# Attention feeding a SwiGLU block: the combined tile half a group later, q and k by DMA from tile 9, a new pace for attention

## The chip, the cores and the metric

The kernel runs on one core of a Trainium2 chip. The metric is device time in microseconds (us) of one execution, lower is better. Where a few tenths matter I also quote the mean granted TensorE clock of a run: a run at a mean clock of 0.99 is not the same run as one at 1.00.

## The reference, cut to what matters

Eight batches of eight heads, 576 positions, head size 64. Attention looks back over a window of 128 positions with a linear bias; its output, 4608 tokens of 512 values, goes through a gated feed-forward block.

```python
def _attn_ref(q, k, v):                       # (8, 8, 576, 64) each
    scores = scale * np.matmul(q, k.transpose(0, 1, 3, 2))
    bias = slopes[:, None, None] * (-np.abs(rel))[None, :, :]
    mask = (rel >= 0) & (rel < 128)
    scores = np.where(mask, scores + bias[None], -1e9)
    ...                                       # softmax over the keys
    return np.matmul(attn, v)

def _moe_ref(x, w_gate, w_val, w_out):        # x (4608, 512), 512 -> 1536 -> 512
    g = x @ w_gate
    silu = g * (1.0 / (1.0 + np.exp(-g)))
    return silu * (x @ w_val) @ w_out
```

## The kernel before: the parts concerned

The work is one stream of TensorE (PE) instructions in which attention and feed-forward are interleaved. Two batches form a group `s`. A group has eight whole tiles of 128 rows (p = 0 to 7) and one *combined* tile (p = 8) that holds the last 64 rows of both batches. Attention makes the tiles in the order of `units`; the feed-forward block takes them 512 rows at a time (blocks 0 to 7, and block 8 of the four combined tiles).

```python
QK_DMA_FROM = 14                 # q and k of tiles from here on are transposed by DMA
...
units = [(s, p) for s in range(NSUP) for p in range(9)]
...
def transpose(n):
    name, rank = order[n]
    if rank < QK_DMA_FROM:
        transposed(name, rank)   # 4 PE transposes and a copy by VectorE or ScalarE
        return
    t_ = (natk if name == "k" else natq).pop(rank)
    nc.sync.dma_start_transpose(transposed_home(name, rank), t_.rearrange("p h d -> p (h d)"))
```

The scores of tile p take its own keys against its own queries and those of the next tile, so scores of (1,0) need q of two tiles:

```python
nc.tensor.matmul(two[par][:, j, :], kT[rows, ks, pair, :],
                 qT[rows, p:p + 2, pair, :], start=(j == 0), stop=(j == 1))
```

Loads of q, k and v are issued by GpSimd into one queue, through a ring of four buffers each for q and k (`nat`, `bufs=4`). A load waits for the transpose that reads its buffer. The two halves of the output weight (768 KB each) stand in the same queue, behind tile 8.

How far attention runs is set by the step of the feed-forward block:

```python
for step in steps:
    if step < 24:
        blk, target = 0, base + max(0, step - ALONE) + 2 * max(0, step - 16)
    else:
        blk = min(NBLK - 1, 1 + int((step + LEAD - 24) // 34.5))
        target = base + 32 + (step - 24) * RATE * 8 / 34.5
    while (n_att < target or done < ready[blk]) and att_step():
        pass
```

The softmax here doesn't subtract the row's maximum and nothing guards it: scores larger than these inputs give would overflow.

## Time and profile before

| what | before |
|---|---|
| time, median of 3 runs | 361.49 us |
| span of the profiled run | 359.7 us, mean clock 0.997 |
| PE busy | 343.1 us (95%) |
| idle PE between 27 and 351 us | 6.6 us |
| longest PE wait after the start | 1.49 us, at 54.43 us, just before block 1 |

The lines behind this table stand in the prediction. The row of slices for the granted clock (40 slices of 9.0 us, a 9 is 90% or more): full until the drain. PE's timeline: start, duration, engine, line, operation, and in brackets the idle time before it with what ended it.

```profile
PEclk9999999999999999999999999999999999999998
```

### The profile page before, as it was taken

How to read it: one execution, taken by the hardware profiler on the slowest of the kernel's cores; microseconds unless marked ns; L12 is line 12 of the kernel's file. 1: busy time of each engine (PE TensorE's matmuls, PEld its weight loads, DVE VectorE, ACT ScalarE, POOL GpSimd, SP SyncE). 2: the span in 40 equal slices, each digit the busy share in tenths (PEclk: the TensorE clock that was granted, in tenths of full speed). 3: DMA queues.
4: the chain of work that ended last, by engine and by line, in shares of the span. 5: the costliest groups of instructions: out<-in, count | busy, mean ns of one | idle time of the engine just before them, and what ended most of it. 6: DMA issues, size and time to landing. Idle time of an engine off the chain costs nothing.

```text
span 359.7 us, 7185 instructions
## 1 busy us (share of the span) xinstructions
PE 343.1 (95%) x2741; PEld 196.1 (55%) x2741; DVE 273.9 (76%) x599; ACT 180.3 (50%) x356; POOL 106.8 (30%) x132
## 2 busy tenths in 40 slices
PE   7888989999999999999999999999999999999995
PEld 3654445444556655565566655564565566456543
DVE  4748975987987799768977998789877955975540
ACT  4837675456755555456565454555454333333321
POOL 8954778325153165463560001000000000000000
PEclk9999999999999999999999999999999999999998
DMA  9999999969999999999999303220031101101113
GB/s 149 171 187 186 172 178 149 134 46 112 107 119 98 110 117 136 185 170 142 175 179 175 89 18 29 84 78 16 15 76 55 49 10 51 58 2 59 60 25 93
DMA packets 154499, 36.55 MB, mean 102 GB/s; under 512 B 144992, under 2 KB 149984, under 8 KB 154464
## 3 DMA queue, kind: packets, MB, share of 16 engines
q0 software_dynamic: 116224, 18.62, 79.6%
q1 hardware_dynamic: 37792, 17.18, 24.6%
q8 instruction: 21, 0.34, 0.4%
q10 hardware_dynamic: 448, 0.30, 0.3%
q14 instruction: 14, 0.11, 0.1%
HBM read 37.91 MB, written 9.44 MB: 132 GB/s over the span
## 4 chain that ended last, share of the span: by engine, by line
PE 72%; DVE 8%; DMA 7%; ACT 5%; POOL 4%; issue 3%; ACTq 0%; DVEq 0%; POOLq 0%
PE pg L361 21%; PE pv L361 21%; PE po L470 14%; PE av L312 4%; DMA qn<-in_q_dram 4%; PE po L391 3%; PE ps L252 3%; PE p L470 2%; DMA wv_sb<-in_moe_w_val_dram 2%; PE px L338 2%; DVE uu L374 2%; ACT ex L257 1%; DVE hT L378 1%; ACT tt L372 1%; PE psc L280 1%
## 5 line engine op out<-in xcount | busy, mean ns | idle before, releaser
L372 ACT ACTIVATE tt<-pg 128x512 f16<-128x512 f32 x108 | 64.8, 602 | 112.8 <-PE pg L361 104.9
L361 PE MATMUL pg<-xT,wg_sb 128*128 128x512 f16 (+2 forms) x444 | 114.9, 373 | 1.0 <-ACT xT L339 0.7
L361 PE MATMUL pv<-xT,wv_sb 128*128 128x512 f16 (+2 forms) x444 | 113.6, 373 | 0.5 <-DVE uu L374 0.5
L374 DVE SCALAR_TENSOR_TENSOR uu<-tt,pg 128x512 f16<-128x512 f16 x107 | 73.0, 683 | 34.8 <-ACT tt L372 34.6
L378 DVE TENSOR_TENSOR hT<-uu,pv 128x512 f16<-128x512 f16 x108 | 73.7, 683 | 6.9 <-PE pv L361 3.9
L361 PEld LDWEIGHTS <-wg_sb 128*128 128x128 f16 x444 | 41.7, 98 | 40.2 <-issue 3.8
L361 PEld LDWEIGHTS <-wv_sb 128*128 128x128 f16 x444 | 41.0, 98 | 35.4 <-issue 3.1
L257 ACT ACTIVATE ex<-ps 128x512 f16<-128x512 f32 x96 | 50.4, 608 | 10.9 <-PE ps L252 10.8
L172 POOL DMA_DIRECT2D qn<-in_q_dram x39 | 33.3, 858 | 40.9 <-DMA qT<-qn 34.3
L166 POOL DMA_DIRECT2D va<-in_v_dram x40 | 34.0, 857 | 35.5 <-PE av L312 27.4
L172 POOL DMA_DIRECT2D kn<-in_k_dram x39 | 33.2, 854 | 32.6 <-DMA kT<-kn 25.2
L470 PEld LDWEIGHTS <-hT 128*128 128x128 f16 x336 | 32.0, 98 | 15.5 <-issue 2.3
L261 DVE TENSOR_TENSOR ex<-ex,m_reg 128x1024 f16<-128x1024 f16 x48 | 32.7, 687 | 7.5 <-ACT ex L257 7.2
L470 PEld LDWEIGHTS <-S 128*128 128x128 f16 x252 | 23.9, 98 | 13.4 <-issue 4.9
L315 DVE TENSOR_TENSOR x<-av,rec 128x256 f16<-128x256 f32 x72 | 29.0, 420 | 0.8
L470 PE MATMUL po<-T,S 128*128 128x256 f16 x168 | 23.1, 273 | 0.1
L470 PE MATMUL po<-T,hT 128*128 128x256 f16 x168 | 22.9, 272 | 0.2 <-DVE osb L474 0.2
L284 ACT ACTIVATE exc<-psc 128x512 f16<-128x512 f32 x40 | 21.2, 608 | 3.3 <-PE psc L280 3.3
L312 PE MATMUL av<-va,ex 128*128 128x65 f16 x384 | 20.7, 193 | 1.8 <-DVE x L315 1.3
L312 PEld LDWEIGHTS <-ex 128*128 128x128 f16 x384 | 18.1, 97 | 6.0 <-DVE x L315 2.0
L339 ACT COPY xT<-px 128x512 f16<-128x512 f16 x24 | 14.0, 584 | 13.7 <-PE px L338 13.3
L391 PE MATMUL po<-wo_sb,hT 128*128 128x512 f16 x84 | 20.7, 379 | 0.0
(72 smaller groups left out, 295.6 us busy)
## 6 DMA issues: line engine op xcount, KB each, us to landing
out_dram<-osb SPq DMA_DIRECT2D x32, 256.0 KB, 2.2
va<-in_v_dram POOLq DMA_DIRECT2D x32, 128.0 KB, 7.7
qn<-in_q_dram POOLq DMA_DIRECT2D x31, 128.0 KB, 6.7
kn<-in_k_dram POOLq DMA_DIRECT2D x31, 128.0 KB, 6.3
wo_sb<-in_moe_w_out_dram POOLq DMA_DIRECT2D x2, 768.0 KB, 9.1
wg_sb<-in_moe_w_gate_dram POOLq DMA_DIRECT2D x2, 512.0 KB, 10.6
wv_sb<-in_moe_w_val_dram POOLq DMA_DIRECT2D x2, 512.0 KB, 12.3
out_dram<-osb SPq DMA_DIRECT2D x6, 128.0 KB, 2.3
```

The source lines that it names most:

```text
L166: nc.gpsimd.dma_start(va[rank][p0:p1, :, 0:D], src)
L172: nc.gpsimd.dma_start(t_[p0:p1], src)
L257: nc.scalar.activation(e[:, o:o + 2, :], banks[q4][par], AF.Exp, scale=scale)
L261: nc.vector.tensor_mul(e[:, o, :], e[:, o, :], reg[:, o, :])
L312: nc.tensor.matmul(av[:, j, :], w, val, start=(n == 0), stop=(n == len(todo) - 1))
L315: nc.vector.tensor_mul(x[:, 4 * half:4 * half + 4, :], av[:, :, 0:D], rec.broadcast_to([P, 4, D]))
L361: nc.tensor.matmul(ps[:, c0:c1], w[:, kb, ms], xT[n][:, kb, c0:c1], start=(kb == 0 and c0 == 0), stop=(kb == NKB - 1 and c1 == 512))
L372: nc.scalar.activation(tt, pg, AF.Tanh, scale=0.5)
L374: nc.vector.scalar_tensor_tensor(out=uu, in0=tt, scalar=one if (n, m) == PIN else 1.0, in1=pg, op0=ALU.add, op1=ALU.mult)
L378: nc.vector.tensor_mul(hT[n][:, m, :], uu, pv)
L391: nc.tensor.matmul(po, hT[n][:, m, j * P:(j + 1) * P], wo_sb[:, m, :], start=(i == 0), stop=(i == NMB - 1))
L470: nc.tensor.matmul(dst, a[:, m, cols], b[:, m, :], start=(start and m == 0), stop=(m == HM - 1), skip_group_check=True)
```

## The change

There are four intentions in it. (1) The combined tile of a group moves half a group later, so that block 2 waits for 12 attention tiles instead of 13. (2) q and k of tiles 9 to 13 are transposed by DMA instead of PE, as all later tiles already are. (3) One quarter of block 0's projection (12 matmuls) is put ahead of block 1, as filler, and the rest is spread. (4) Attention gets an even pace in stretches. The rest (homes of the tiles in the rings, shared masks, lists of what is needed when) follows from (1).

```diff
-QK_DMA_FROM = 14
+QK_DMA_FROM = 9
+PRE = 1
+SECOND = 5
...
-    NK, NQ = 12, 9
+    NK, NQ = 14, 10
...
-    opool = ctx.enter_context(tc.tile_pool(name="op", bufs=8))
+    opool = ctx.enter_context(tc.tile_pool(name="op", bufs=7))
...
-    units = [(s, p) for s in range(NSUP) for p in range(9)]
+    units = [(0, p) for p in range(8)]
+    for s in range(1, NSUP):
+        units += [(s, 0), (s, 1), (s, 2), (s, 3), (s - 1, 8), (s, 4), (s, 5), (s, 6), (s, 7)]
+    units += [(NSUP - 1, 8)]
...                                 (homes in the rings, masks, order of the transposes)
+            if n == 1:
+                for j in range(PRE):
+                    for _ in project(0, j, ps_f, "po", 1):
+                        yield 1.0
...
-                    if 1 <= m <= 4:
-                        for _ in project(0, m - 1, ps_f, "po", 1):
+                    if m % 2 and PRE + m // 2 < 4:
+                        for _ in project(0, PRE + m // 2, ps_f, "po", 1):
...
-    ready = [4, 8, 13, 17, 22, 26, 31, 35, 36]
+    ready = [4, 8, 12, 17, 21, 26, 30, 35, 36]
...
-            if step < 24:
-                blk, target = 0, base + max(0, step - ALONE) + 2 * max(0, step - 16)
+            b1 = 24 + 3 * PRE
+            blk = (0 if step + LEAD < b1 else 1 if step + LEAD < 60
+                   else min(NBLK - 1, 2 + int((step + LEAD - 60) // 34.5)))
+            if step < b1:
+                target = base + 32 * max(0, step - ALONE) / (b1 - ALONE)
+            elif step < 60:
+                target = base + 32 + SECOND * 8 * (step - b1) / (60 - b1)
             else:
-                blk = min(NBLK - 1, 1 + int((step + LEAD - 24) // 34.5))
-                target = base + 32 + (step - 24) * RATE * 8 / 34.5
+                target = base + 32 + SECOND * 8 + (step - 60) * RATE * 8 / 34.5
```

Tile numbers count along `units`. In the order of before, tile 8 is the combined tile (0,8) and tile 9 is (1,0). In the new order tile 8 is (1,0), tile 9 is (1,1) and the combined tile (0,8) is tile 12.

More of the change, by code (lines that the diff above doesn't have):

```diff
@@ L97 @@
     nc.vector.memset(idle, 0.0)
-    msk = [consts.tile([P, H, P], FP16, name=f"m_c{n}") for n in range(3)]
-    nc.vector.memset(msk[0][:, :, 64:128], 0.0)
-    nc.vector.memset(msk[1][:, :, 0:64], 0.0)
+    band = consts.tile([P, H, 192], FP16, name="m_band")
+    msk = [band[:, :, 64:192], band[:, :, 0:128], consts.tile([P, H, P], FP16, name="m_own")]
+    nc.vector.memset(band, 0.0)
     nc.vector.memset(msk[2], 0.0)
     def make_masks():
-        nc.scalar.copy(msk[0][:, :, 0:64], reg[:, :, 128:192])
-        nc.scalar.copy(msk[1][:, :, 64:128], reg[:, :, 128:192])
+        nc.scalar.copy(band[:, :, 64:128], reg[:, :, 128:192])
         nc.scalar.copy(msk[2][0:64, :, 0:64], reg[0:64, :, 0:64])
@@ L140 @@
         va_all += [tv[:, 0], tv[:, 1]]
-    units = [(s, p) for s in range(NSUP) for p in range(9)]
+    units = [(0, p) for p in range(8)]
+    for s in range(1, NSUP):
+        units += [(s, 0), (s, 1), (s, 2), (s, 3), (s - 1, 8), (s, 4), (s, 5), (s, 6), (s, 7)]
+    units += [(NSUP - 1, 8)]
+    rank_of = {u: i for i, u in enumerate(units)}
     last = len(units) - 1
@@ L149, with home @@
     natq, natk, va = {}, {}, {}
+    def home(name, s, c):
+        if name == "q":
+            return c if c < 8 else 8 + s % 2
+        if c in (3, 7, 8):
+            return 8 + 3 * (s % 2) + (3, 7, 8).index(c)
+        return (6 * s + (0, 1, 2, 4, 5, 6).index(c)) % 8
     def transposed_home(name, rank):
-        return kT[:, rank % NK] if name == "k" else qT[:, rank % NQ]
+        return (kT if name == "k" else qT)[:, home(name, *units[rank])]
     def source(src, rank):
-        s, c = divmod(rank, 9)
+        s, c = units[rank]
         if c == 8:
@@ L163, in load_v @@
     def load_v(rank):
-        va[rank] = va_all[rank % NV]
+        va[rank] = va_all[home("v", *units[rank])]
         for (p0, p1), src in source(v, rank):
@@ L204, in transposed @@
             nc.vector.tensor_copy(transposed_home(name, rank), pt)
-    order = []
-    for s in range(NSUP):
-        for half in (0, 4):
-            order += [(name, 9 * s + half + r) for name, r in zip("kqqkqkqk", (0, 0, 1, 1, 2, 2, 3, 3))]
-        order += [("k", 9 * s + 8), ("q", 9 * s + 8)]
-    need = [18 * s + n for s in range(NSUP) for n in (3, 5, 7, 8, 11, 13, 15, 18, 18)]
+    order, need = [], []
+    for i, (s, p) in enumerate(units):
+        wanted = [("k", s, p), ("q", s, p)] + ([("q", s, p + 1)] if p not in (3, 7, 8) else [])
+        if i < last and units[i + 1][1] == 8:
+            wanted += [("k", units[i + 1][0], 8), ("q", units[i + 1][0], 8)]
+        order += [w for w in ((n, rank_of[(s_, c)]) for n, s_, c in wanted) if w not in order]
+        need.append(len(order))
     def transpose(n):
@@ L226, in scores, with combined @@
         s, p = units[i]
-        def combined(n):
+        def combined(s, n):
             return scores_128(s, (3, 7, 8)[n], 8, (s, "c", n), msk[n])
@@ L233, in scores @@
         if p == 8:
-            return together(combined(1), combined(2))
-        if p == 7:
-            return together(scores_128(s, p, p, (s, p), reg[:, :, 0:P]), combined(0))
-        if p == 3:
-            return scores_128(s, p, p, (s, p), reg[:, :, 0:P])
-        ks = (9 * s + p) % NK
+            return together(combined(s, 1), combined(s, 2))
+        if p in (3, 7):
+            own = scores_128(s, p, p, (s, p), reg[:, :, 0:P])
+            follows = i < last and units[i + 1][1] == 8
+            return together(own, combined(units[i + 1][0], 0)) if follows else own
+        ks = home("k", s, p)
         banks = []
@@ L266, in scores_128 @@
     def scores_128(s, kt, qt, key, m):
-        ks = (9 * s + kt) % NK
+        ks, qs = home("k", s, kt), home("q", s, qt)
         banks = []
@@ L279, in products @@
                     rows = slice(64 * par, 64 * par + 64)
-                    nc.tensor.matmul(banks[par][:, j, :], kT[rows, ks, j, :], qT[rows, qt, j, :],
+                    nc.tensor.matmul(banks[par][:, j, :], kT[rows, ks, j, :], qT[rows, qs, j, :],
                                      start=(j == 0), stop=(j == 3))
@@ L304, in weighted @@
                     for n, kt in enumerate((3, 7, 8)):
-                        todo.append((j, ex[(s, "c", n)][:, slot(h), :], va[9 * s + kt][:, h, :]))
+                        todo.append((j, ex[(s, "c", n)][:, slot(h), :], va[rank_of[(s, kt)]][:, h, :]))
                 else:
@@ L308, in weighted @@
                         todo.append((j, ex[(s, p - 1)][:, slot(h), 128:256],
-                                     va[9 * s + p - 1][:, h, :]))
-                    todo.append((j, ex[(s, p)][:, slot(h), 0:128], va[9 * s + p][:, h, :]))
+                                     va[rank_of[(s, p - 1)]][:, h, :]))
+                    todo.append((j, ex[(s, p)][:, slot(h), 0:128], va[rank_of[(s, p)]][:, h, :]))
             for n, (j, w, val) in enumerate(todo):
```

## The prediction

> **What bounds the kernel now.** I read the page's first table first, then the slices, then the busy time by stretches, then the waits, and last the timeline of the stretch in which the stretches showed a loss.
>
> ```profile
> PE 343.1 (95%) x2741; PEld 196.1 (55%) x2741; DVE 273.9 (76%) x599; ACT 180.3 (50%) x356; POOL 106.8 (30%) x132
> ...
> DMA  9999999969999999999999303220031101101113
> ```
>
> TensorE is busy 343.1 of 359.7 us, so 16.6 us is all that visible idle time could give. The second line shows where another limit stands: the DMA engines are full for the first half of the run. The stretches say where the 16.6 us lie (columns: stretch, its length, busy PE, PEld, DVE, ACT, POOL, then granted clock, DMA share, GB/s):
>
> ```profile
> 0.00:27.00 27.00, 21.25 (x237) 14.19 (x238) 14.69 (x45) 14.26 (x29) 22.19 (x31) 1.00 1.86 169
> 27.00:54.00 27.00, 24.06 (x204) 12.02 (x201) 23.10 (x47) 19.85 (x39) 17.22 (x22) 1.00 1.86 179
> 54.00:72.00 18.00, 17.36 (x146) 9.03 (x147) 13.89 (x32) 9.06 (x17) 11.19 (x13) 1.00 2.38 141
> 72.00:276.00 204.00, 201.37 (x1668) 115.47 (x1667) 170.89 (x378) 111.80 (x223) 56.17 (x68) 1.00 1.08 101
> 276.00:351.00 75.00, 74.57 (x463) 42.39 (x462) 50.92 (x101) 24.37 (x47) 0.00 (x0) 1.00 0.13 43
> ```
>
> Idle PE: 5.75 us before 27 us (the start, which the change hardly touches), 2.94 from 27 to 54, 0.64 from 54 to 72, 2.63 in the next 204, 0.43 in the next 75, and 4.5 in the drain. So from 27 us on the change can win at most 6.6 us of visible idle time, and none of it for sure. The one large piece is here, at the end of block 0, just before block 1 may begin:
>
> ```profile
> 52.13 0.81 PE L361 MATMUL pv<-xT,wv_sb 128*128 128x512 f16 x3
> 54.43 0.28 PE L338 MATMUL px<-idm,x 128*128 128x128 f16 x2 [1.49 <-DVE x L315]
> ```
>
> PE stands 1.49 us waiting for the attention tile that completes block 1's input. The diff aims at this: it gives attention an even pace and puts 12 projection matmuls of block 0 behind it as filler. In the same stretch the loads are one full queue:
>
> ```profile
> va<-in_v_dram POOLq DMA_DIRECT2D x9, 128.0 KB, 7.6
> kn<-in_k_dram POOLq DMA_DIRECT2D x4, 128.0 KB, 7.1
> qn<-in_q_dram POOLq DMA_DIRECT2D x3, 128.0 KB, 7.6
> ```
>
> These are the DMA issues from 36 to 60 us: 7 us from issue to landing for 128 KB, because each stands behind its predecessors. The trace's own record has one load landing about every 1.0 us from 37 to 65 us, and one half of the output weight about every 3.6 us.
>
> **What the skill says.** (1) "VectorE: DVE Perf Modes", section "The three transpose paths": a 128x128 transpose takes 390 ns on TensorE and 1309 ns by DMA. The trace has other sizes: on PE, four 128x128 transposes start within 0.22 us (0.055 us each in the stream), and a tile of q or k by DMA (four such blocks) takes 2.4 to 7.6 us from issue to landing. As latency the DMA path is far slower; as PE time it is free. (2) "DMA: Bandwidth & Descriptors", section "SWDGE vs HWDGE vs iDMA": each DMA engine round-robins between the queues of the two kinds, so a transpose issued by SP shares the engines with the loads issued by GpSimd. The trace agrees: transposes alone took 2.4 to 2.5 us, one with loads in flight 5.5 us (the one issued at 86.8 us), another 7.6 us. (3) "TensorE: Matmul & The Clock Gate", section "What's actually happening": one idle window of about 3.4 us puts the PE clock back to half. Before, no idle time after the start is over 1.5 us, and the granted clock reads 1.00 until 351 us, so the trace does not test it; in the changed kernel it may.
>
> ```profile
> L220 SPq DMA_TRANSPOSE qT<-qn x1: 1191/1191/1191, 86.8 to 86.8; - x1
> ...
> DMA to landing us min/median/max: 5.5/5.5/5.5
> ```
>
> **The change part by part.** Building both shows PE with 40 matmuls fewer and no other count changed on it.
>
> - *q and k of tiles 9 to 13 by DMA.* 5 tiles x 2 x 4 = 40 transposes leave PE: 40 x 0.055 = 2.2 us of stream time, all on the bounding engine, with perhaps 0.3 us of turn-around. 5 copies of 0.42 us leave DVE and 5 of 0.59 us leave ACT; both have slack over most of the run, so I give nothing for that. 10 DMA transposes are added, in a stretch where the DMA is full.
> - *Combined tile later.* The 16 narrow score matmuls, the masks and the four half loads of combined tile (0,8) leave the rush before block 2, and block 2 now needs 12 attention tiles done and not 13. No PE work is saved. The sequence of PE shows block 1's first matmul after 40.4 us of pure stream time (each matmul at its undisturbed start-to-start distance) and not 41.6.
> - *Projection ahead, pacing.* No work saved; it can close the 1.49 us hole and about 1 us of smaller ones up to 60 us.
> - *Masks.* One ACT copy of 0.62 us less in the first block, a longer memset on DVE in the first 3 us, beside the first loads. Nothing.
>
> If nothing else happened the sum would be 2.2 + 0.3 + 2.5 + about 1 for the later holes, or 6 us: 355.5 us.
>
> **The step that I think takes most of it back.** In the changed order PE meets the scores of tile (1,0) right after 36.6 us of stream time, still before block 1; before, that place held the scores of the combined tile, whose q and k came by PE. Tile (1,0) needs q of tile 9, which now comes by DMA: that matmul has a wait for the first DMA transpose, and PE runs its matmuls in order. When does q9 arrive? The order of the loads up to index 32 of the DMA queue is unchanged in bytes, and that one landed at 41.1 us before. Behind it in the new order stand two v tiles (1.1 + 1.05), both halves of the output weight (3.5 + 3.8), k8, q8 and q9 (0.95 each): 41.1 + 2.15 + 7.3 + 2.85 = 53.4 us (estimate from the landings of before). Then the transpose, with five or six loads still in flight: 2.5 us if it were alone, 5.5 as at 86.8 us, or 7.6. I take 5: q9 is usable at 58.4 us. PE gets to that matmul at about 53 us, since the place with the same stream work was reached at 54.4 before, and q8's own landing (52.4) holds it no longer than that. So PE stands about 5 us, and then is 58.4 - 54.4 = 4.0 us behind the kernel before at equal work. Later transposes have time: k9 and q10 should be there by 61 us and are wanted after 62; q11 and k10 by 70, wanted near 75.
>
> Sum: 361.5 + 4.0 (q9) - 2.5 (transposes left after that place) - 2 (holes after 54 us closed, since DVE and ACT catch up during the stall and the pace is even) + 0.8 (half clock after a 5 us stall: 1.7 us if it comes, at a chance of about one half) = 361.8. As the constants of the change look tuned, I shade this a little: **361.0 us**.
>
> **Rivals.**
> (a) *The transpose is quick enough, or PE gets there later.* Then the holes close as intended and the kernel gains 4 to 7 us: 354.5 to 357.5. For it: lone transposes at 2.4 us; with that, q9 is there at 55.9 and the loss against before is 1.5 us. Against it: the full DMA row from 36 to 60 us, and that the first transpose took 4.1 us even with no load in flight.
> (b) *Stall and cold clock at full size.* q9 at 60 to 61 us and half clock for a window or two: 366 to 368. For it: 7.6 us was seen with five loads in flight. Against: block 1's work was not DMA-bound before, and the stall lets DVE empty its queue.
> (c) *Nothing but the PE sum matters.* PE stays the bound, the hole only moves: 359. For it: 72 to 276 us has only 2.6 us of idle PE, so pace can't matter much there.
> (d) *Loads become the pace later*: in the new order the load of q11 reuses the buffer of q9 and waits for its transpose, so GpSimd stands still until 58 us. GpSimd already waited 34.3 us in all for such transposes without hurting PE, so I give this little.
>
> ```profile
> POOL qn L172 <- DMA qT<-qn: 34.3, 8, 9.7
> ```
>
> **Range and chances.** The middle is between (c) and the stalled sum; (a) gives the low end, 356, and a stall with some cold clock the high end, 366. Faster by over 2% means under 354.3, which needs (a) with all holes closed: 0.07. Slower by over 2% means over 368.7, which needs (b) and more: 0.05. Within 2%: 0.88.
>
> **What would show it.** Right: PE groups with 108 half-precision q/k transposes and not 148; an idle stretch of 3 to 7 us on PE before the scores of tile (1,0), ended by the DMA transpose of q, between 55 and 61 us, with the chain of waits running through that transpose and a load of q; PE idle from 72 to 276 us at 2.6 us or less. Wrong: that wait under 1.5 us (then rival (a) and a time near 356), or new waits of PE for DMA after 70 us (rival (d)), or a granted clock under 1.00 after the stall for more than 4 us (rival (b)).

## More of the kernel before

```profile
37.67 0.40 PE L199 MATMUL pt<-idm,qn 128*128 128x128 f16 x4 [0.18 <-DMA qn<-in_q_dram]
```

The transposes of a q tile at 37.67 us wait only 0.18 us for its load.

## The result, and the profile after

The changed kernel took 364.2 us (median of 363.83, 364.01, 364.40 and 365.02), the kernel before 362.0 us in the same rounds. The ratio is 1.0064, with a 95% interval of 1.0037 to 1.0091. All ratios here are the mean time of one kernel's runs over that of the other's of the same rounds, so not quite the ratio of the medians. All outputs are right. Within 2% it is the same; within its own interval it is 0.6% slower. The profiled run of after is its slowest (365.02 us, span 363.2); that of before took 361.5 us (span 359.7).

First the page of after: the PE row, and the rows of slices for the granted clock and the DMA engines.

```profile
PE 342.0 (94%) x2701; PEld 195.1 (54%) x2701; DVE 272.5 (75%) x593; ACT 177.5 (49%) x350; POOL 106.8 (29%) x132
...
PEclk9999996999999999999999999999999999999999
DMA  9999999999999999799999700211221101101104
```

PE has 40 matmuls fewer, as predicted, and the busy time is down by only 1.1 us. The seventh slice of the clock row, 54.5 to 63.6 us, has a 6 where before had a 9: PE ran part of it at half clock. The DMA row is full up to the 22nd slice in both kernels but for one slice each (before's is in the prediction): the loads are one long queue here as there.

The busy time of after by stretches (columns as in the prediction) puts the loss in one place:

```profile
27.00:54.00 27.00, 23.55 (x199) 11.72 (x196) 22.57 (x46) 18.53 (x36) 13.25 (x16) 1.00 1.87 180
54.00:72.00 18.00, 13.72 (x78) 6.39 (x79) 8.37 (x18) 5.84 (x11) 7.32 (x9) 0.81 1.67 103
72.00:276.00 204.00, 200.27 (x1666) 114.94 (x1664) 172.04 (x381) 110.94 (x222) 63.69 (x77) 1.00 1.26 110
276.00:351.00 75.00, 74.68 (x480) 42.79 (x479) 54.43 (x107) 25.70 (x50) 0.00 (x0) 1.00 0.12 41
```

From 54 to 72 us PE is idle 4.28 us (before 0.64), at a mean clock of 0.81, and does 78 matmuls where before did 146. From 27 to 54 us it is idle 3.45 us (before 2.94), from 72 to 276 us 3.73 us (before 2.63). The timeline of PE shows the two waits behind the first two of these:

```profile
37.50 0.40 PE L214 MATMUL pt<-idm,qn 128*128 128x128 f16 x4 [1.96 <-DMA qn<-in_q_dram]
...
53.93 0.29 PE L354 MATMUL px<-idm,x 128*128 128x128 f16 x2
58.24 1.04 PE L268 MATMUL ps<-qT,kT 64*128 64x256 f16 x8 [4.03 <-DMA qT<-qn]
...
60.79 1.90 PE L407 MATMUL po<-wo_sb,hT 128*128 128x512 f16 x4
```

The matmuls at 58.24 us are the scores of tile (1,0), the first that need a q by DMA (q9). PE stood 4.03 us for them. The last line shows the clock: four 512-column matmuls in 1.90 us; the same four take 1.03 us at full clock. The first line is the place where the even pace went: attention now begins its q transposes earlier in PE's stream than the load is there, and waits 1.96 us instead of 0.18. So the 1.49 us hole of before is gone (no wait at 53.93), but 1.78 us of new wait stands at an earlier load.

The chain of waits of after in order of time (start, duration, what), around the stall:

```profile
52.28 0.07 PE pg L377
52.36 5.75 DMA qT<-qn
58.11 0.14 issue
58.24 0.63 PE ps L268 x4
```

It runs through that transpose. Its own start is set by the load of q9: in the trace's records that load landed at 52.27 us and the transpose was issued at 52.36. The chain puts another name there, which ended at the same moment. The load and the transpose, as tiles:

```profile
L187 POOL DMA_DIRECT2D qn<-in_q_dram x2: 873/882/890, 39.1 to 39.9; - x2
...
DMA to landing us min/median/max: 12.3/12.3/12.4
```

```profile
L236 SPq DMA_TRANSPOSE qT<-qn x1: 1302/1302/1302, 52.4 to 52.4; - x1
...
  POOL qn L187: 7.1, 1
  PE ps L268: 4.0, 1
...
DMA to landing us min/median/max: 5.8/5.8/5.8
```

q9 was issued at 39.9 us and took 12.3 us to land, because it stands behind the output weight. Its transpose took 5.75 us beside the loads that follow.

**The ledger.** To add the terms up I split the time from PE's first to its last matmul in both traces. Each matmul has an undisturbed distance to the next start, read from full-clock stretches (0.2155 us for 512 columns, 0.108 for 256, 0.0557 for 128, 0.029 for 65). Two score matmuls that start together count as one. Their sum is the *stream*; what a distance has beyond that is *excess*: waiting, half clock, and also a fixed extra at a change of shape (in before most 512-column matmuls ahead of a pair of 256-column scores have 0.312 us to the next start and not 0.2155), so it is more than idle time.

| us | before | after | after, kept warm (e4) |
|---|---|---|---|
| stream | 317.73 | 315.50 | 319.38 (3.88 of it dummies) |
| excess up to the first matmul of block 0 | 9.93 | 9.88 | 9.72 |
| excess from there to the first of block 1 | 7.36 | 13.60 | 7.65 |
| excess in blocks 1 to 8 | 19.03 | 19.11 | 19.12 |

So after lost 4.0 us to PE's last matmul: -2.23 stream, +6.24 in block 0, +0.08 later, -0.05 at the start. Its drain was 0.5 us shorter, which gives the 3.5 us between the spans. The 6.24 us in block 0 are the 4.03 us wait for q9, 2.07 us of half clock (from e4, below), and 0.14 us of the rest, in which the closed hole (-1.49) and the longer wait at 37.5 us (+1.78) nearly cancel.

### The profile page after: what moved, and what is told of

Read it like the earlier page. It is cut to its first block, busy times and chain, and to the rows that moved or that the text cites.

```text
span 363.2 us, 7118 instructions
## 1 busy us (share of the span) xinstructions
PE 342.0 (94%) x2701; PEld 195.1 (54%) x2701; DVE 272.5 (75%) x593; ACT 177.5 (49%) x350; POOL 106.8 (29%) x132
## 4 chain that ended last, share of the span: by engine, by line
PE 63%; DVE 15%; DMA 8%; ACT 5%; issue 4%; POOL 3%; ACTq 0%; DVEq 0%; POOLq 0%
PE pg L377 19%; PE pv L377 18%; PE po L486 12%; PE po L407 4%; DMA qn<-in_q_dram 4%; PE av L328 3%; DVE uu L390 3%; DVE hT L394 3%; PE p L486 2%; DMA wv_sb<-in_moe_w_val_dram 2%; ACT ex L273 2%; PE ps L268 2%; DVE ex L277 2%; ACT tt L388 2%; DMA qT<-qn 2%
## 5 line engine op out<-in xcount | busy, mean ns | idle before, releaser
L390 DVE SCALAR_TENSOR_TENSOR uu<-tt,pg 128x512 f16<-128x512 f16 x107 | 73.1, 684 | 34.7 <-ACT tt L388 34.3
L486 PEld LDWEIGHTS <-S 128*128 128x128 f16 x252 | 23.8, 98 | 12.3 <-issue 4.1
L268 PE MATMUL ps<-qT,kT 64*128 64x256 f16 x192 | 17.1, 278 | 5.3 <-DMA qT<-qn 4.0
## 6 DMA issues: line engine op xcount, KB each, us to landing
wv_sb<-in_moe_w_val_dram POOLq DMA_DIRECT2D x2, 512.0 KB, 12.3
```

Source lines behind the costliest of these rows:

```text
L268: nc.tensor.matmul(two[par][:, j, :], kT[rows, ks, pair, :], qT[rows, p:p + 2, pair, :], start=(j == 0), stop=(j == 1))
L390: nc.vector.scalar_tensor_tensor(out=uu, in0=tt, scalar=one if (n, m) == PIN else 1.0, in1=pg, op0=ALU.add, op1=ALU.mult)
L486: nc.tensor.matmul(dst, a[:, m, cols], b[:, m, :], start=(start and m == 0), stop=(m == HM - 1), skip_group_check=True)
```

## The experiments

**Theory A** (that of the prediction): the stall for q9 and the half clock after it are the loss; the rest of the change is neutral to good. **Rival B**: the loss is the half clock alone or mostly, so a warm PE would do. **Rival C**: the new order, the pace and the projection are worth nothing or less by themselves, and there was no gain to lose. **Rival D**: loads and transposes become the pace, and removing one wait moves it to the next.

Every kernel ran beside the kernel before. e1 to e4 ran on one chip with 3 rounds (before: median 363.15 us), e5 to e8 on a second with 5 rounds (before: 362.32), e9, e10 and e12 on a third with 5 rounds (before: 362.50), e13 on the second again (before: 362.41). The runs of before scatter from 361.2 to 366.4 us, and their mean clock goes with it: 361.2 to 361.6 us at a mean clock of 0.997 to 1.000, and 366.4 at 0.984.

| run | order | q, k by DMA from | pace, projection | median us | ratio to before [95%] | us at a mean clock of 0.997 or more |
|---|---|---|---|---|---|---|
| before | old | 14 | old | 362.3 to 363.2 | 1 | 361.2 to 361.6 |
| e12 | old | 11 | old | 361.13 | 0.9970 [0.9931, 1.0008] | 359.6 |
| e3 | old | 9 | old | 361.34 | 0.9933 [0.9863, 1.0003] | none |
| e10 | old | 14 | new | 361.68 | 0.9983 [0.9957, 1.0009] | 361.7 |
| e9 | old | 11 | new | 360.73 | 0.9951 [0.9927, 0.9974] | 360.5 |
| e6 | old | 9 | new | 360.26 | 0.9939 [0.9912, 0.9966] | 358.9, 359.4 |
| e2 | new | 14 | new | 362.33 | 0.9978 [0.9920, 1.0035] | 362.1 |
| e7 | new | 13 | new | 362.32 | 1.0003 [0.9978, 1.0028] | 362.0 to 362.5 |
| e8 (= after) | new | 9 | new | 364.43 | 1.0062 [1.0035, 1.0089] | none |

The last column rests on few runs: eleven of before, four of e7, two each of e12, e10, e9 and e6, one of e2. It compares kernels at equal clock, and so leaves out what a change does to the chance of half clock.

### e1: tile 9 by PE

```diff
-QK_DMA_FROM = 9
+QK_DMA_FROM = 10
```
(after, otherwise unchanged)

> The changed kernel with one edit: q and k of tile 9 are transposed by TensorE again, tiles 10 to 13 stay on DMA (8 transposes back on PE, 0.45 us of stream). Theory A (the 4.03 us wait for the DMA transpose of q of tile 9, and the half clock from 58.1 to 64.9 us that follows it, are what eats the gain): no wait over 1.5 us near 54 to 58 us, clock 1.00 throughout, and 364.2 - 3.8 - 3.2 + 0.45 = 357.6 us. Rival B (the stall only takes up slack: the loss lies in the later order, pace or DMA crowding): within 1.5 us of the changed kernel, 363 to 365.

It took 367.21 us, ratio 1.0107 [1.0043, 1.0171]: no better than after (1.0064 [1.0037, 1.0091]), and whether it is worse the intervals don't settle. The stall for q9 was gone, but PE's timeline of e1 has it again 28 us later:

```profile
81.36 0.81 PE L407 MATMUL po<-wo_sb,hT 128*128 128x512 f16 x3
85.88 0.90 PE L296 MATMUL psc<-qT,kT 64*128 64x128 f16 x16 [3.71 <-DMA kT<-kn]
86.71 1.89 PE L377 MATMUL pg<-xT,wg_sb 128*128 128x512 f16 x4
```

PE waits 3.71 us for a k by DMA, and the four matmuls after it take 1.89 us, which is half clock again. In the records that k's transpose ran from 78.25 to 85.83 us, and its load had been issued only at 74.06, because GpSimd had stood behind the transpose of a q until 73.09. GpSimd's waits in e1:

```profile
POOL kn L187 <- DMA kT<-kn: 44.1, 13, 8.5
```

The expectation of Theory A was missed by 10 us. Rival D is right in this: loads wait for transposes to free their buffers, transposes wait for loads, and moving one of them moves the wait.

### e2: the new order, pace and projection, with the transposes of before

```diff
-QK_DMA_FROM = 9
+QK_DMA_FROM = 14
```
(after, otherwise unchanged)

> The changed kernel with q and k by DMA only from tile 14 again, so the new place of the combined tile, the projection ahead and the pacing alone. Theory A: no stall, no half clock, 40 transposes back on PE: 364.2 - 7.0 + 2.2 = 359.4 us, so about 2 to 3 us faster than before from order and pace. Rival B: 364 or more, since the order is at fault and 2.2 us of PE work come back. Rival C (order and pace are worth nothing by themselves): 362, as before.

It took 362.33 us, ratio 0.9978 [0.9920, 1.0035], with no stall before block 1. The one run at full clock took 362.09 us, some 0.7 above before's full-clock runs. Theory A wanted 359.4; this is what rival C says. The intent of the change, without the DMA transposes, is worth nothing.

### e3: the kernel before with the transposes of after

```diff
-QK_DMA_FROM = 14
+QK_DMA_FROM = 9
```
(before, otherwise unchanged)

> The kernel before with q and k by DMA from tile 9, nothing else. Theory A: in the old order the first scores that need such a tile come some 9 us of PE stream later (after block 1 has begun), so no wait over 1.5 us there and the 2.2 us of transposes are simply saved: 359.5 to 360. Rival D (ten DMA transposes in a full DMA queue hurt wherever they stand): 362 or more, with a stall of several us between 55 and 75 us.

It took 361.34 us, ratio 0.9933 [0.9863, 1.0003], and its trace has no PE wait for a DMA transpose. All its runs had some half clock (mean 0.986 to 0.995), and it was still below before. So DMA transposes from tile 9 on, which cost 2.1 us in the new order (e8 against e7, below), do no harm here, and by the median help, though the interval includes 1. The difference is what PE meets first: here the combined tile's scores, whose q and k came by PE, stand there; the first scores that need a DMA transpose come after 40.5 us of stream time in e3's trace (63.71 us) and not 36.6. The 9 us of room that were expected were 3.9.

### e4: after, with PE kept warm during the stall

```diff
         def products():
             for q4 in range(2):
                 two = [ps_a.tile([P, 2, 256], FP32, name="ps", tag="a") for _ in range(2)]
                 banks.append(two)
+                if (s, p) == (1, 0) and q4 == 0:
+                    for _ in range(18):
+                        nc.tensor.matmul(two[0].rearrange("p a b -> p (a b)"), idle[:, 0:P], idle,
+                                         start=True, stop=True)
```
(after, with 18 matmuls on zeros into a bank that is overwritten next)

> The changed kernel with 18 dummy matmuls of 512 columns (about 3.9 us) put before the scores of tile (1,0), into the bank that those scores overwrite: PE still may not go on before the DMA transpose of q lands at about 58 us, but is not idle. Theory A with the clock as a cost of its own: granted clock 1.00 throughout, 3.2 us faster than the changed kernel: 361.0. Rival E (the half clock costs nothing, since PE then waits for other engines anyway): no change, 364.

It took 362.82 us, ratio 0.9990 [0.9932, 1.0048]; Theory A had wanted 361.0, since it put the half clock at 3.2 us. The timeline of e4 around the place, and its stretch from 54 to 72 us:

```profile
54.19 4.05 PE L266 MATMUL ps<-kT 128*128 128x512 f16 x18
58.49 0.61 PE L272 MATMUL ps<-qT,kT 64*128 64x256 f16 x8 [0.26 <-DMA qT<-qn]
```

```profile
54.00:72.00 18.00, 17.58 (x108) 7.84 (x107) 10.71 (x23) 8.02 (x16) 7.43 (x10) 1.00 1.66 117
```

The scores start at 58.49 us, still released by the transpose, so the stall itself is unchanged; but the clock is 1.00 and PE does 108 matmuls in the stretch (18 of them dummies) where after did 78. In the ledger, block 0 of after has 13.60 us of excess; e4 has 7.65 and 3.88 of dummies, 11.53 together. The half clock therefore cost 2.07 us, and the wait for q9 the other 4.03. Rival B has a third of the loss; the two together, which is Theory A, have nearly all of it.

### e5: q9 loaded ahead of the output weight

```diff
-    nat = ctx.enter_context(tc.tile_pool(name="nat", bufs=4))
+    nat = ctx.enter_context(tc.tile_pool(name="nat", bufs=6))
...
-    opool = ctx.enter_context(tc.tile_pool(name="op", bufs=7))
+    opool = ctx.enter_context(tc.tile_pool(name="op", bufs=5))
...
     load(8)
-    loaded = 9
+    load_qk(9, "q")
     for a0 in (0, 6):
         nc.gpsimd.dma_start(wo_sb[:, a0:a0 + 6, :], wo2[:, a0:a0 + 6, :])
+    load_qk(9, "k")
+    load_v(9)
+    loaded = 10
```
(after, otherwise unchanged; the fewer output buffers make room)

> The changed kernel with room for six natural q and k tiles in place of four (paid for with two output tiles fewer), and q of tile 9 loaded ahead of the output weight; the PE order is the same, instruction by instruction. If the stall is the landing of q9 plus one transpose, q9 lands near 45 us and not 52.3, its transpose ends near 51, and the 4.03 us wait before the scores of tile (1,0) shrinks to under 1 us. But k9 and q10 still land behind the weight (about 53 and 56 us) and are wanted by the scores of tile (1,1), then at about 58 us: I expect the wait to move there, 2 to 4 us, so 362 to 364 in all. Rival (the wait belongs to the DMA transpose as such, not to the time of the load): the wait stays where it is.

It took 363.92 us, ratio 1.0045 [1.0016, 1.0074]. Timeline, and the transpose of q9:

```profile
54.61 1.01 PE L268 MATMUL ps<-qT,kT 64*128 64x256 f16 x8
...
63.24 0.29 PE L268 MATMUL ps<-qT,kT 64*128 64x256 f16 x2 [4.00 <-DMA qT<-qn]
```

```profile
L236 SPq DMA_TRANSPOSE qT<-qn x1: 1297/1297/1297, 44.6 to 44.6; - x1
...
DMA to landing us min/median/max: 9.2/9.2/9.2
```

The scores of (1,0) at 54.61 us no longer wait. q9 is loaded 7.8 us sooner (44.50 for 52.27 us), its transpose beside the weight load takes 9.2 us, and that is still in time. But the next scores, which need q10, wait 4.00 us, since everything else came as late as before; the half clock followed (63.7 to 67.1 us). The wait is set by the queue of loads and transposes and not by one tile. That is rival D again, and was expected.

### e6: everything of the change but the new place of the combined tile

```diff
 (before, with QK_DMA_FROM = 9, PRE = 1, SECOND = 5 and the three hunks of the
  projection and the pace from the diff above; order, rings and masks as before)
```

> The kernel before with three of the four parts of the change: q and k by DMA from tile 9, one projection of block 0 ahead of block 1, attention paced by stretches; the combined tile stays where it was. If the loss comes from the combination of the new order with DMA from tile 9, this has no wait for DMA before 80 us and saves 2.2 us of transposes and some of the 1.5 us hole: 358.5 to 360 in runs without a half clock, 2 to 3 us under the kernel before in equal clock. Rival: pace or projection ahead are themselves harmful, then it is slower than tile 9 by DMA alone, 361 or more in equal clock.

It took 360.26 us, ratio 0.9939 [0.9912, 0.9966]: the best kernel measured, 0.6% under before, well short of 2%. Its two runs near full clock took 358.9 and 359.4 us. I had expected no DMA wait; the profiled run, its slowest, has one (timeline):

```profile
62.51 0.27 PE L254 MATMUL ps<-qT,kT 64*128 64x256 f16 x1 [2.23 <-DMA qT<-qn]
```

So even the old order has little room between load, transpose and use. It brought no half clock; the stalls that did so elsewhere were 3.71 us or longer.

### e7 and e8: the new order with tile 13 only, and after once more

```diff
-QK_DMA_FROM = 9
+QK_DMA_FROM = 13
```
(e7; e8 is after, unchanged, beside it on the same chip)

> The changed kernel with q and k by DMA from tile 13 only: the first matmul that waits for a DMA transpose comes after 72 us of PE stream and not 36.6. Expected: no wait of PE for DMA over 1 us, 1.8 us of transposes back on PE, the hole before block 1 smaller by 1 us than before: 360 in a run without a half clock, 1.5 us under the kernel before at equal clock, and 2 us under the changed kernel.

> The changed kernel as it is, on this chip and beside the others: the wait of about 4 us ended by the DMA transpose of q near 58 us, and the half clock after it, in each run. The part of each run's time that the mean granted clock explains is taken off to compare: time less (0.997 less the run's mean clock) times its span; that gave 361.0 to 362.1 for seven runs of the kernel before whose plain times were 361.3 to 366.4. I expect 362 +- 0.6 by that measure and 364.2 plain.

e7 took 362.32 us (ratio 1.0003), e8 364.43 us (1.0062 [1.0035, 1.0089]), which repeats the first measurement. Between e8 and e7 only the transposes of tiles 9 to 12 differ: they cost 2.1 us in the new order. For e7 I had expected 360 us, and missed by 2. Its clock was 0.991 to 1.000, so it is not a matter of half clock, and its timeline still has the wait at 37.5 us that the new pace brought, and one for a VectorE copy at the place of the stall:

```profile
37.49 0.40 PE L214 MATMUL pt<-idm,qn 128*128 128x128 f16 x4 [1.88 <-DMA qn<-in_q_dram]
...
55.18 0.61 PE L268 MATMUL ps<-qT,kT 64*128 64x256 f16 x8 [0.75 <-DVE qT L219]
```

e8's expectation compares times "corrected" for the clock. That measure was poor, and I withdraw it: half clock early in the run is partly hidden behind the load that PE waits for at 37.5 us, so correcting for it in full takes off too much from the kernels that had it there. The table above therefore shows runs at full clock instead. After and e8 have no such run: all ten runs have a mean clock of 0.991 (eight of them) or 0.986. One spell of 6.8 us at half clock in a span of 363.2 gives 1 - 0.5 x 6.8 / 363.2 = 0.991. The two traced runs have that spell just after the stall, and the mean clock of the other eight fits it; where theirs lay isn't recorded.

### e9, e10, e12: the parts in the old order

```diff
 e9:   e6 with QK_DMA_FROM = 11
 e10:  e6 with QK_DMA_FROM = 14      (pace and projection alone)
 e12:  before with QK_DMA_FROM = 11  (the transposes alone, of three tiles)
```

> The version that kept the old place of the combined tile, with projection ahead and pacing, and q and k by DMA from tile 11 in place of 9. That version still stood 2.23 us for the DMA transpose of q of tile 10 at 62.5 us; here the first matmul that waits for such a transpose comes after 56.6 us of PE stream and not 40.5. Expected: no wait of PE for a transpose over 0.5 us, 0.9 us of transposes back on PE, so 359.1 - 2.2 + 0.9 = 357.8 us in runs at full clock, and the median 1 us under that version's 360.3. If the wait only moves to a later tile, as it did when tile 9 alone was taken back in the changed kernel: 360 or more.

> The same with q and k by DMA from tile 14, as in the kernel before: projection ahead and pacing alone, in the old order. It tells what these two are worth without any change of the transposes, and, beside the changed kernel from tile 14 (362.1 at full clock), what the new place of the combined tile is worth. If pacing closes the 1.49 us hole and the PE gets there no later: 360.0 at full clock, against 361.4 before; then the new place costs about 2 us. If pacing is worth nothing: 361.4, and the new place costs 0.7.

> The kernel before with q and k by DMA from tile 11 and nothing else. 1.35 us of transposes leave PE (24 of them), and no DMA transpose is wanted before 54 us of PE stream: 360.0 at full clock. Beside the version with projection ahead and pacing from tile 11 it tells what these two add: 2 us if they close the hole, none if not.

e10, the pace and the projection alone, takes 361.7 us at full clock: the time of before. Yet it does what it was written for. Timelines at the place of the 1.49 us hole, e10 first, then e12:

```profile
55.80 0.29 PE L340 MATMUL px<-idm,x 128*128 128x128 f16 x2 [0.29 <-DVE x L317]
```

```profile
54.35 0.28 PE L338 MATMUL px<-idm,x 128*128 128x128 f16 x2 [1.49 <-DVE x L315]
```

In e10 the hole is 0.29 us; in e12, which keeps the old pace, it is still 1.49. And e12 at full clock is 2.1 us *faster* than e10 (359.6 and 361.7). In a ledger of e10 made like the one above, the excess in block 0 is 8.00 us against 7.36 before, in spite of the closed hole, at the start 10.30 against 9.93, and later 18.35 against 19.03. But e10's trace has half clock from 20.5 to 23.9 us, which before's has not, and part of the 8.00 is that. Where the closed hole went in e10's full-clock runs this ledger can't show. A candidate is the wait for the load at 37.5 us: 1.88 us in e7 (the same pace in the new order, its trace at full clock) and 0.18 in before.

e9 missed its 357.8 us: 360.5 at full clock, where e12 with the same transposes and the old pace has 359.6. Here the new pace costs 0.9 us. No PE wait in e9's trace for a DMA is over half a microsecond, but that trace has half clock from 21.5 to 24.9 us, behind which a wait at 37.5 us can hide. I have no run that says where the 0.9 goes; that stays open.

### e13: e3 with filler at the start

```diff
             av = pool.tile([P, 4, D + 1], FP32, name="av", tag=tag)
+            if 0 < i < FIRST:
+                for _ in range(3):
+                    nc.tensor.matmul(av.rearrange("p a b -> p (a b)"), idle[:, 0:P],
+                                     idle[:, 0:4 * (D + 1)], start=True, stop=True)
```
(e3, with 18 matmuls on zeros in the first tiles, to prevent half clock there)

> The kernel before with q and k by DMA from tile 9, plus 18 dummy matmuls of 260 columns in the gaps of the first four attention tiles (15 to 21 us, where some runs of every kernel fall to half clock for one or two spells of 3.4 us). Expected if the scatter of runs is that clock: nearly all runs at a mean clock of 0.997 or more, median 359.3 us, 0.9 per cent under the kernel before of the same rounds. If the fillers delay the start instead: 360.5 or more at full clock. If the old order does not bear DMA from tile 9: a wait of PE for a transpose near 60 us.

It took 360.79 us, ratio 0.9968 [0.9939, 0.9997]; 359.3 was expected. The half clock at the start was gone in the trace, but its runs at full clock took 360.6 to 361.1 us, so it missed; that the filler costs about what it saves is likely and not shown, since e3 has no run at full clock. And the profiled run had half clock elsewhere, from 56.45 to 59.86 us. The stretch of e13 from 54 to 60 us and the 3.42 us just before the spell, then e2 from 15 to 27 us (spell from 18.25 to 25.08):

```profile
54.00:60.00 6.00, 5.48 (x46) 3.09 (x47) 3.60 (x10) 2.56 (x5) 0.86 (x1) 0.72 1.76 123
53.03:56.45 3.42, 1.94 (x23) 1.12 (x23) 2.34 (x7) 1.49 (x4) 0.00 (x0) 1.00 2.52 160
```

```profile
15.00:27.00 12.00, 9.94 (x97) 6.33 (x95) 6.18 (x20) 4.61 (x9) 8.41 (x11) 0.72 1.61 191
```

The granted clock was 0.72 in both, though no single idle time in the first was over 1.5 us. PE's high busy time there (5.48 of 6 us) is partly the spell itself, in which matmuls take double time; in the 3.42 us before the spell PE was idle 1.48. That is the 1.49 us hole of the old pace, which e3 and e13 have whole just before such a spell; before and e12 have the hole and no spell. Spells of 3.4 or 6.8 us stand in ten of the 14 traces taken, and in six of them at the start (18 to 28 us), so not in every kernel as the expectation has it. In all ten PE was idle at least 36% of the 3.41 us before each spell, but that alone does not set one off: after was idle 46% of the time from 33.54 to 36.95 us and kept full clock. The mean clocks of the runs without a trace, before's included, fall with their times, which fits the same cause for the scatter of 361 to 366 us. The runs don't settle what sets a spell off.

## Why the prediction was right, and which terms were off

The class, the range and the mechanism of the stall held: the same within 2%, 364.2 us in a range of 356 to 366. The middle, 361.0, was 3.2 us too low, and the sign of the small difference was wrong. By the steps:

- **The transposes left PE.** Predicted -2.2 us of stream; measured -2.23, with 40 matmuls fewer. The extra 0.3 for turn-around can't be told apart from the rest.
- **The stall before the scores of (1,0).** Named as the step that takes the gain back, and right in cause, place and order of size: 4.03 us for the predicted 5. The estimate for q9 (landed 53.4, transpose 5, usable at 58.4) compares with 52.27, 5.75 and 58.11. Two errors of about 1 us cancelled, which was luck. "PE gets to that matmul at about 53 us" was 54.2.
- **The lag at equal work.** Predicted 4.0 us; 58.24 against 54.43 is 3.8. Right. It made no difference to it that the hole of 1.49 us was gone and a wait of 1.96 us at 37.5 us had come: after the stall PE's place is set by q9 and not by what PE did before.
- **Half clock, 0.8 us.** Mis-sized: this was 1.7 us times a chance of one half. It came in both traced runs, for 6.8 us (57.4 to 64.3), the mean clock of the other eight fits it, and it cost 2.07 us. The loss was about right (2.07 for 1.7), by luck: 1.7 is half of a spell of 3.4 us, and this one was twice as long. The chance was not right. That is +1.3 us. By the prediction's own list this was also a sign of being wrong: more than 4 us under full clock was to speak for rival (b).
- **"2 us of holes after 54 us closed."** This term failed. The excess in blocks 1 to 8 went from 19.03 to 19.11 us: nothing was closed. The sign named for it failed too: PE idle from 72 to 276 us is 3.73 us where 2.6 or less was to show. e10 says why it was a poor term: pace and projection alone, with no stall in the way, left the time at 361.7. The filler was not new either: the prediction overlooked the 14 projection matmuls that before already ran ahead of block 1. That is +2.1 us.
- **The sum.** 361.8 was the sum and 361.0 after the shade. With the two terms corrected, 361.8 + 1.3 + 2.1 = 365.2, against 365.0 of the profiled run. The shade, "as the constants of the change look tuned", had no ground in the profile and went the wrong way by 0.8.
- **Rivals.** (a) was out: the wait was 4.03 us. (b) named half clock of a full window or two and was right in that; its size, 366 to 368, was too much because q9 was there at 58.1 and not at 60 to 61. (c), nothing but the PE sum, 359, was wrong for after, yet e10 and e2 show its premise right: pace is worth nothing here. (d) was right more than I gave it: in after GpSimd waits more and PE has no DMA wait past 70 us, but e1 and e5 show that the queue of loads and transposes is the limit just behind the stall.

GpSimd's waits of after, to be held against the 34.3 us of before in the prediction:

```profile
POOL qn L187 <- DMA qT<-qn: 40.0, 11, 8.4
```

What is shown and what is not. Shown are: that the DMA transposes are the one part that pays in the old order (e6, whose interval against before is under 1 where that of e10 is not; 359.2 against 361.7 us at full clock, on two chips on which before agrees; e12 at full clock; the intervals of e12 and e3 alone include 1), that they cost 2.1 us in the new order (e8 against e7), and that the stall and the half clock add up to this loss (e4, ledger). That the new place of the combined tile causes it by bringing the first DMA-fed scores forward is shown by e6 against e8, which differ in this and what follows from it: 360.26 and 364.43 us on the same chip. Why the new order costs 0.4 us even without DMA transposes (e2, 362.1, against e10, 361.7), and why the new pace costs 0.9 us in e9 against e12, stays open; both are near the scatter.

## What to carry to other kernels

Before moving work from the bounding engine to DMA, find the first consumer in that engine's order and add up when its data can be there, in the queue as it is loaded then; a reordering that is harmless by itself can bring that consumer forward, and then one late tile costs more than all the instructions saved. The stall of 4 us on TensorE cost more than its length, here half as much again: all four traced stalls of 3.71 to 4.21 us (e1, e5, after, e8) brought half clock, so count it in for a stall of that length. And a hole in the timeline is not sure to be worth its length: this one closed in e10 and gained nothing at full clock, and in the changed kernel a wait of the same size appeared at an earlier load.

## What the Trainium skill lacked or had wrong

- "VectorE: DVE Perf Modes", section "The three transpose paths", gives 1309 ns for a 128x128 transpose by DMA and says nothing of one beside other transfers. The tile of four such blocks took 2.4 to 4.1 us with no load in flight (before), and 5.75 us (after) and 9.2 us (e5) beside loads in the other queue. The loaded figure decides whether the path can be used.
- "DMA: Bandwidth & Descriptors", section "Anatomy of one DMA — SWDGE (gpsimd) path", fits one DMA as about 2.0 us plus bytes over 436 KB per us, which would be an estimated 2.3 us for 128 KB. In a full queue the load of q9 took 12.3 us from issue to landing, because the output weight stood before it. The page's figure is for a DMA by itself, which no run here tests; in a queue that is kept full, the bytes ahead set the time.
- "TensorE: Matmul & The Clock Gate", section "What's actually happening", has half clock after an idle window of about 3.4 us. The stalls of 4.03 us (after), 4.21 us (e8), 4.00 us (e5) and 3.71 us (e1) agree. But half clock came too where no idle time was near that: 56.4 to 59.9 us in e13, with a longest idle time of 1.49 us and PE idle 1.48 of the 3.42 us before it. The section "A second HAM failure mode: psum-queue depth-cycling" tells of frequent short idle times doing this, without a threshold; the runs here don't give one either.
